# Finer pieces in an instruction planner, first scores in two PSUM banks behind products of ones, and embeddings taken first

## Chip, cores and metric

The kernel runs on one core of a Trainium2 chip. The metric is the device time of one execution in microseconds (us), the median of three runs; less is better. TensorE (PE in the profile) multiplies matrices, VectorE (DVE) and ScalarE (ACT) work on vectors, GpSimd (POOL) and SyncE (SP) mostly start transfers.

## What is computed

Three stages on 4608 tokens of 512 numbers. The first is attention between `x` (8 batches, 8 heads, 512 positions, 64 numbers) and a small `state` (32 positions), read in both directions. The second is a feed-forward layer with a squared ReLU. The third sends each token to one of 8 experts and scales the result by a softmax weight.

```python
scores = scale * np.matmul(x, state.transpose(0, 1, 3, 2))
a = softmax(scores);  xread = np.matmul(a, state)
scores2 = scale * np.matmul(state, x.transpose(0, 1, 3, 2))
a2 = softmax(scores2);  sread = np.matmul(a2, x)
tok = concatenate([xread, sread])            # 8 x (512 + 32) tokens of 512
h = relu(tok @ w_in);  y = (h * h) @ w_out   # 512 -> 2048 -> 512
logits = norm(y) @ norm(expert_emb).T / tau
e = argmax(logits);  gate = softmax(logits)[e]
out = gate * (relu(y @ w1[e]) @ w2[e])       # 512 -> 1024 -> 512
```

`w_in` and `w_out` arrive as 64-bit floats and are turned into 32-bit ones in the kernel.

## The kernel before, in words

Every product that decides the routing has to be more exact than one 16-bit product, so most operands are split into a high and a low 16-bit half and multiplied as high-high, high-low, low-high.

**Decoding.** `w_in` and `w_out` come in 16 blocks (`block`, eight of each). A block is 1 MB of 64-bit numbers. `to_f32` decodes it with one instruction of 1024 elements on ACT (L882) and three on DVE (L885, L887, L894); `wi_scale` squares a `w_in` block on ACT (L911), sums the squares with four products with a matrix of ones (`oneb`, L919) and takes a power-of-two scale from the sum (L925, L932). Two blocks give one quarter of `w_in`.

**Attention of batch 0** (`first_attention`, `first_scores`, `first_scale`). It starts before any weight is there. `first_scores` multiplies two halves of `x` with the state, both into one PSUM tile `S` (L597, eight 32-bit products for a half, each issued as two passes with a weight load each). `weigher` makes the softmax: row maxima (L519), subtraction (L521), exponential on ACT (L528), sum (L530), three small steps, multiplication (L536), a cast on ACT (L540), the low half (L542), and a transposing DMA (L549). `state_side` does the other direction (L750 and on).

**Hidden layer.** For batch b, `first_state_w` or `state_w` multiplies the state with a quarter of `w_in` (L649, L686) and splits the result into `sw` (L659 on ACT, L316 on DVE). `up1` multiplies `sw` with the transposed softmax (L1349 to L1351, twelve products of 256 columns for a hidden unit, in a ring of two PSUM tiles `u`); `hidden` reads `u` on ACT (L1302), squares it and splits it. `down1` multiplies the hidden values with `w_out`: for the first two token groups in 32 bits (L1412, 16 products for each of 4 tiles, so 64; it can begin before the halves of `w_out` exist), later in 16-bit halves (L1433 to L1435). It has a ring of two PSUM tiles `d`: the first two tiles must be read by `route_tile` (L1173, then L321 and L316) before the third begins.

**Order.** Nothing is scheduled by a compiler. Each piece of work is a Python generator that yields requests such as `"pe", 1.2` (engine, duration), events, or slots. `Plan.run` keeps a clock for each engine, takes again and again the request that can start first (ties go to the lower priority number), and lets that generator write its instructions. Each engine then executes its list strictly in order. After a request a generator's own time is the end plus `LAT`:

```python
dep = r[2] if len(r) > 2 else th[2]
key = (max(dep, self.free[r[0]]), th[1])
th[2] = start + dur + self.LAT
```

So the size of a request sets how finely two products' lists can be mixed: `down1` asks for four 32-bit products (which the planner counts as 16; the trace shows two passes for each), or for twelve 16-bit ones, in one request.

**Embeddings.** `embeddings` normalises the expert embeddings: 22 small DVE instructions (L1138 to L1159), one of them behind four small products (L1146). It starts after `wo scale`, that is after all 16 blocks are decoded. Its two inputs are loaded by `prepare` on SP's queue.

## Time and profile before

| | |
|---|---|
| median of 3 runs | 1090.7 us (1090.12 to 1091.49) |
| the profiled execution, its own time | 1089.88 us |
| its span, first to last instruction | 1088.1 us |
| PE busy | 1039.9 us (96%) |
| DVE busy | 684.6 us (63%) |
| ACT busy | 588.2 us (54%) |

The profile gives for each engine what it executed and when. A row of the timeline has the start, the duration, the engine, the line, what is written from what, and in brackets how long the engine was idle before and what ended that. [...]

### The profile page before, as it was taken

The numbers are of one execution on the slowest core, as the hardware profiler recorded it, in microseconds if no ns is written. First come the engines' busy times: TensorE is split into PE (matmuls) and PEld (weight loads), VectorE is DVE, ScalarE is ACT, GpSimd is POOL, SyncE is SP. The second block draws the span as 40 slices with busy tenths as digits, with TensorE's granted clock in tenths as the row PEclk, the third lists the DMA queues.
The fourth block names the chain that finished last, engine by engine and source line by source line (L and its number), as shares of the span: only waits on it lengthen the run. The fifth ranks groups of instructions, "written<-read, shape, count | busy, mean of one in ns | idle before, by whom it ended". The sixth has DMA issues, their size and how long they took to land. (4 is left out here: it accounts for less than half of the span.)

```text
span 1088.1 us, 26339 instructions
## 1 busy us (share of the span) xinstructions
PE 1039.9 (96%) x10657; PEld 672.2 (62%) x10657; DVE 684.6 (63%) x1787; ACT 588.2 (54%) x976; POOL 124.3 (11%) x149
## 2 busy tenths in 40 slices
PE   4679999999999999999999999999999999999997
PEld 3345446565656566565555666677677777767774
DVE  5788798868878778887797784466322323222222
ACT  4778779787887988887787984211110101111110
POOL 0000000200101001002002020312122121212111
PEclk8799999999999999999999999999999999999999
DMA  6873144874875565887559587753898777694691
GB/s 216 288 248 110 60 97 146 233 209 133 242 226 150 153 181 173 233 210 217 166 162 262 194 262 246 218 138 80 277 285 166 195 226 219 169 292 141 182 311 69
DMA packets 161311, 211.74 MB, mean 195 GB/s; under 512 B 112225, under 2 KB 114529, under 8 KB 155938
## 3 DMA queue, kind: packets, MB, share of 16 engines
q1 hardware_dynamic: 152866, 182.94, 58.2%
q0 software_dynamic: 8320, 27.08, 8.2%
q8 instruction: 85, 1.39, 0.5%
q14 instruction: 40, 0.33, 0.1%
HBM read 257.92 MB, written 51.68 MB: 285 GB/s over the span
## 5 line engine op out<-in xcount | busy, mean ns | idle before, releaser
L1699 ACT ACTIVATE r<-u 128x512 f32<-128x512 f32 x70 | 41.8, 597 | 319.5 <-PE u L1745 288.7
L1433 PE MATMUL d<-wo_t,g 128*128 128x512 f16 x480 | 182.1, 379 | 1.0 <-DVE g L1319 1.0
L1435 PE MATMUL d<-wo_t,g 128*128 128x512 f16 x480 | 182.1, 379 | 0.2
L1434 PE MATMUL d<-wo_t,g 128*128 128x512 f16 x480 | 182.1, 379 | 0.0
L1349 PE MATMUL u<-aT,sw 128*128 128x256 f16 x512 | 141.3, 276 | 9.7 <-ACT r L1302 7.6
L1351 PE MATMUL u<-aT,sw 128*128 128x256 f16 x512 | 141.0, 275 | 0.2 <-DVE sw L316 0.2
L1350 PE MATMUL u<-aT,sw 128*128 128x256 f16 x512 | 141.0, 275 | 0.0
L1702 DVE CAST hh<-r 128x512 f16<-128x512 f32 x70 | 29.9, 428 | 127.8 <-ACT r L1699 126.3
L1302 ACT ACTIVATE r<-u,cg 128x512 f32<-128x512 f32 x120 | 81.5, 680 | 47.9 <-PE u L1351 27.2
L1713 DVE TENSOR_SCALAR o<-d,rec,wo_t 128x512 f32<-128x512 f32 x35 | 28.3, 810 | 111.0 <-PE d L1768 108.5
L1275 POOL DMA_INDIRECT rec_d<-rec,pi x34 | 38.5, 1132 | 519.9 <-DVE is L301 140.8
L1768 PEld LDWEIGHTS <-hh 128*128 128x128 f16 (+1 forms) x688 | 54.7, 103 | 57.6 <-issue 1.3
L1321 DVE TENSOR_TENSOR g<-r,g 128x512 f16<-128x512 f32 x120 | 82.2, 688 | 7.5 <-ACT r L1316 5.9
L1435 PEld LDWEIGHTS <-g 128*128 128x128 f16 x480 | 46.9, 98 | 57.7 <-DVE g L1321 1.2
L1743 PE MATMUL u<-xes,stage 128*128 128x128 f16 x448 | 75.9, 219 | 0.0
L1745 PE MATMUL u<-xes,stage 128*128 128x128 f16 x448 | 75.9, 219 | 0.0
L1744 PE MATMUL u<-xes,stage 128*128 128x128 f16 x448 | 75.9, 219 | 0.0
L1433 PEld LDWEIGHTS <-g 128*128 128x128 f16 x480 | 47.2, 98 | 46.3 <-DVE g L1319 1.9
L1316 ACT ACTIVATE r<-r 128x512 f32<-128x512 f32 x120 | 74.5, 626 | 1.4
L1434 PEld LDWEIGHTS <-g 128*128 128x128 f16 x480 | 46.9, 98 | 44.2
L1743 PE MATMUL u<-xes,xx 128*128 128x128 f16 x416 | 70.5, 220 | 0.0
L1744 PE MATMUL u<-xes,xx 128*128 128x128 f16 x416 | 70.4, 219 | 0.0
(338 smaller groups left out, 2637.7 us busy)
## 6 DMA issues: line engine op xcount, KB each, us to landing
w_d<-he SPq DMA_DIRECT2D x128, 256.0 KB
g<-w_d SPq DMA_DIRECT2D x16, 2048.0 KB
wo_t<-w_d SPq DMA_DIRECT2D x16, 2048.0 KB
stage<-w_d SPq DMA_DIRECT2D x14, 2048.0 KB
he<-w_d SPq DMA_DIRECT2D x14, 2048.0 KB
xx<-w_d SPq DMA_DIRECT2D x13, 2048.0 KB
sw<-w_d SPq DMA_DIRECT2D x13, 2048.0 KB
stage<-in_w_dram SPq DMA_DIRECT2D x20, 1024.0 KB
```

The costliest lines, as they stand in the source:

```text
L1302: nc.scalar.activation(out=r, in_=ps, func=AF.Relu, scale=cg[:, g:g + 1] if u >= F32U else cgq[:, c:c + 1])
L1316: nc.scalar.activation(out=r, in_=r, func=AF.Square)
L1321: V.tensor_tensor(out=gl, in0=r, in1=gh, op=ALU.subtract)
L1349: mm(o, lhsT=hl[:, i, 0, fs], rhs=aT[:, i, :], start=i == 0, stop=False)
L1350: mm(o, lhsT=hl[:, i, 0, fs], rhs=aT[:, 2 + i, :], start=False, stop=False)
L1351: mm(o, lhsT=hl[:, i, 1, fs], rhs=aT[:, i, :], start=False, stop=i == 1)
L1433: mm(ps, lhsT=g_h[:, f, ts], rhs=w[:, 0, :], start=f == 0, stop=False)
L1434: mm(ps, lhsT=g_h[:, f, ts], rhs=w[:, 1, :], start=False, stop=False)
L1435: mm(ps, lhsT=g_l[:, f, ts], rhs=w[:, 0, :], start=False, stop=f == KF - 1)
L1743: mm(p[:, j, xs], lhsT=w[:, 0, k, fs], rhs=xe[:, k, xs], start=k == 0, stop=False)
L1744: mm(p[:, j, xs], lhsT=w[:, 0, k, fs], rhs=xe[:, 4 + k, xs], start=False, stop=False)
L1745: mm(p[:, j, xs], lhsT=w[:, 1, k, fs], rhs=xe[:, k, xs], start=False, stop=k == 3)
```

## The change

It does these things, all of them before or around the first 130 us of the program, and by the planner everywhere:

- `Plan`: a request of a generator for the same engine as its last one is no longer delayed by `LAT`; the DMA queue is taken to begin at 1.2.
- `down1` asks for its products in pieces: a quarter of what it asked for at a time, in both forms.
- `first_attention` issues five products of a 128x128 matrix of ones with 512 columns of ones before it waits for the state, and four more before the scores (`warm`), into one of the `d` tiles, which it releases again.
- `first_scores` puts the two halves into two tiles of the `u` ring instead of the one tile `S`; `weigher` takes the tile and a function that releases it.
- `embeddings` is started at the program's begin, loads its inputs on ACT's queue ahead of everything else there, and asks for its DVE work in six pieces.
- The priority of `first_scale` goes from 0.95 to 1.2.

```diff
--- before.py
+++ after.py
@@ -115,12 +115,12 @@
 
     def __init__(self):
         self.free = dict.fromkeys(("pe", "act", "dve", "pool", "sp"), 0.0)
-        self.dma_free = 0.0
+        self.dma_free = 1.2
         self.threads = []
         self.cur = None
 
     def add(self, gen, prio):
-        th = [gen, prio, self.cur[2] if self.cur else 0.0, None]
+        th = [gen, prio, self.cur[2] if self.cur else 0.0, None, None]
         self.threads.append(th)
         was, self.cur = self.cur, th
         self._advance(th)
@@ -141,10 +141,13 @@
 
     def _advance(self, th):
         was, self.cur = self.cur, th
+        at = th[2]
         try:
             th[3] = next(th[0])
         except StopIteration:
             self.threads.remove(th)
+        if th[2] != at:
+            th[4] = None
         self.cur = was
 
     def run(self):
@@ -163,7 +166,7 @@
                         self._advance(th)
                         break
                 else:
-                    dep = r[2] if len(r) > 2 else th[2]
+                    dep = r[2] if len(r) > 2 else th[2] - (self.LAT if r[0] == th[4] else 0)
                     if r[0] == "pe" and 1.3 <= th[1] < 5:
                         dep += self.MARGIN
                     key = (max(dep, self.free[r[0]]), th[1])
@@ -174,7 +177,7 @@
                 (start, _), th, dep = best
                 eng, dur = th[3][0], th[3][1]
                 self.free[eng] = start + dur
-                th[2] = start + dur + self.LAT
+                th[2], th[4] = start + dur + self.LAT, eng
                 self._advance(th)
 
 
@@ -502,13 +505,12 @@
                 ss_ = slice(sb * 128, sb * 128 + 128)
                 for n, (a, w) in enumerate(pairs):
                     mm(o, lhsT=w[:, c, ss_], rhs=a[:, c, :], start=n == 0, stop=n == 2)
-        w = weigher(b, Sp, xh, xl, scl, 0, 32)
-        yield from w
-
-    def weigher(b, Sp, xh, xl, scl, m0, m1):
+        S4 = Sp.rearrange("p a (h n) -> p (a h) n", n=NS)
+        yield from weigher(b, S4, xh, xl, scl, 0, 32, s_slots.release)
+
+    def weigher(b, S4, xh, xl, scl, m0, m1, read):
 
         ms, n = slice(m0, m1), NS * (m1 - m0)
-        S4 = Sp.rearrange("p a (h n) -> p (a h) n", n=NS)[:, ms]
         mx = small.tile([128, 32], F32, name="mx")[:, ms]
         e1 = xh.rearrange("p c s -> p (c s)").bitcast(F32).rearrange("p (m n) -> p m n", n=NS)
         a16 = xl.rearrange("p c s -> p (c s)").rearrange("p (t c m n) -> p t m c n", t=2, c=4, n=NS)
@@ -519,11 +521,7 @@
         V.tensor_reduce(out=mx, in_=S4, axis=X, op=ALU.max)
         yield dve(n)
         V.tensor_tensor(out=e1, in0=S4, in1=mx.unsqueeze(2).to_broadcast([128, m1 - m0, NS]), op=ALU.subtract)
-        ev("S read", b, m1).set()
-        if m1 == 32:
-            if m0:
-                yield ev("S read", b, m0)
-            s_slots.release()
+        read()
         yield act(n)
         nc.scalar.activation(out=e1, in_=e1, func=AF.Exp, scale=scl)
         yield dve(n)
@@ -559,6 +557,16 @@
 
     def first_attention():
 
+        yield d_slots
+        idle, k_d = ps_d.tile([128, 512], F32, name="d"), d_slots.last()
+
+        def warm(n):
+            yield "pe", 0.25 * n
+            for _ in range(n):
+                mm(idle.rearrange("p (a n) -> p a n", a=4), lhsT=oneb, rhs=oneb.unsqueeze(1).to_broadcast([128, 4, 128]),
+                   start=True, stop=True)
+
+        yield from warm(5)
         yield ev("st", 0)
         stt = st_t.pop(0)
         yield xhl_slots
@@ -571,11 +579,13 @@
         yield "pe", 0.2
         mm(p[:, 2:3], lhsT=one32, rhs=ss[:, 2:3], start=True, stop=True)
         mm(p[:, 256:512], lhsT=oneb, rhs=xl.bitcast(BF16)[:, :, :64], start=True, stop=True)
-        yield s_slots
-        Sp = ps_s.tile([128, 4, 256], F32, name="S")
+        at = plan.now()
+        yield from warm(4)
+        d_slots.release(k_d)
+        plan.cur[2] = at
         for t in range(2):
-            plan.add(first_scores(t, Sp, xh, xl, stt), 0.4 + 0.1 * t)
-        plan.add(first_scale(ss, stt), 0.95)
+            plan.add(first_scores(t, xh, xl, stt), 0.4 + 0.1 * t)
+        plan.add(first_scale(ss, stt), 1.2)
         v = small.tile([128, 2], F32, name="sv")[:, 0:1]
         yield tiny(4)
         V.tensor_scalar(out=v, in0=p[:, 2:3], scalar1=FLOOR, scalar2=None, op0=ALU.max)
@@ -588,16 +598,22 @@
         plan.add(first_state_w(stf), 0.6)
         plan.add(group_bound(0, p), 0.7)
 
-    def first_scores(t, Sp, xh, xl, stt):
+    def first_scores(t, xh, xl, stt):
         yield ev("first x", t)
         xf = xf_t[0, 0]
-        yield "pe", 2.0
-        for sb in (2 * t, 2 * t + 1):
+        at = plan.now()
+        yield u_slots
+        plan.cur[2] = max(at, plan.now())
+        Sp, k_h = ps_u.tile([128, 512], F32, name="u").rearrange("p (a n) -> p a n", a=2), u_slots.last()
+        yield "pe", 1.9
+        for a in range(2):
+            sb = 2 * t + a
             for c in range(4):
-                mm(Sp[:, sb, c * 64:c * 64 + 64], lhsT=xf[:, c, sb * 128:sb * 128 + 128], rhs=stt[:, c, :],
+                mm(Sp[:, a, c * 64:c * 64 + 64], lhsT=xf[:, c, sb * 128:sb * 128 + 128], rhs=stt[:, c, :],
                    start=True, stop=True)
         ev("scored", t).set()
-        yield from weigher(0, Sp, xh, xl, eighth, 16 * t, 16 * t + 16)
+        S4 = Sp.rearrange("p a (h n) -> p (a h) n", n=NS)
+        yield from weigher(0, S4, xh, xl, eighth, 16 * t, 16 * t + 16, lambda: u_slots.release(k_h))
 
     def first_scale(ss, stt):
 
@@ -1132,10 +1148,13 @@
         ev("experts").set()
 
     def embeddings():
-        yield ev("wo scale")
-        yield ev("prepared")
-        yield "dve", 3.0
+        yield "act", 1.0
+        nc.scalar.dma_start(emf, embT)
+        nc.scalar.dma_start(tsb, tau.to_broadcast([128, 1]))
+        plan.cur[2] += 2.5
+        yield tiny(1)
         V.reciprocal(out=itau, in_=tsb)
+        yield tiny(2)
         V.tensor_scalar(out=itau, in0=itau, scalar1=float(2.0 ** -14), scalar2=None, op0=ALU.mult)
         e2 = small.tile([128, 4, NE], F32, name="emq", bufs=1)
         V.tensor_tensor(out=e2, in0=emf, in1=emf, op=ALU.mult)
@@ -1144,12 +1163,16 @@
         yield "pe", 0.4
         for k in range(4):
             mm(p[:, 0:NE], lhsT=one32, rhs=e2[:, k, :], start=k == 0, stop=k == 3)
-        yield tiny(20)
+        yield tiny(1)
         v = small.tile([128, NE], F32, name="env", bufs=1)
         V.tensor_scalar(out=v, in0=p[:, 0:NE], scalar1=FLOOR, scalar2=None, op0=ALU.max)
         t_slots.release()
         y = small.tile([128, NE], F32, name="eny", bufs=1)
+        yield tiny(5)
+        yield tiny(6)
         rsqrt(y, v, NE)
+        yield tiny(4)
+        yield tiny(4)
         V.tensor_tensor(out=y, in0=y, in1=v, op=ALU.mult)
         V.tensor_scalar(out=y, in0=y, scalar1=1e-6, scalar2=None, op0=ALU.add)
         V.reciprocal(out=y, in_=y)
@@ -1406,9 +1429,9 @@
             for q in range(NB):
                 yield ev("f32", q)
                 yield ev("g", u, q)
-                yield pe(16, 512)
                 for i in range(2):
                     for f in range(2):
+                        yield pe(4, 512)
                         mm(pair[i][0], lhsT=g32[:, i, 2 * q + f, 128 * u:128 * u + 128], rhs=wo32[q][:, f, :],
                            start=q + f == 0, stop=q == NB - 1 and f == 1)
                 ev("down32", u, q).set()
@@ -1427,8 +1450,8 @@
                     if u == F32U:
                         for a in (2 * q, 2 * q + 1):
                             yield ev("wo", a)
-                    yield pe(12, 512)
                     for f in range(4 * q, 4 * q + 4):
+                        yield pe(3, 512)
                         w = wo[f // 2][:, :, f % 2, :]
                         mm(ps, lhsT=g_h[:, f, ts], rhs=w[:, 0, :], start=f == 0, stop=False)
                         mm(ps, lhsT=g_h[:, f, ts], rhs=w[:, 1, :], start=False, stop=False)
@@ -1820,9 +1843,8 @@
         yield from load(cs, cst, 1 << 17)
         yield from load(cs16, cst16, 1 << 16)
         yield from load(rid, rowid, 1 << 15)
-        yield from load(tsb, tau.to_broadcast([128, 1]), 512)
-        t = yield from load(emf, embT, 1 << 14)
-        yield "pool", 1.0, t
+        t = plan.now()
+        yield "pool", 1.0, t + 2.0
         dz = mg.tile([128, REC], F32, name="rec0", bufs=1)
         nc.gpsimd.memset(dz, 0.0)
         nc.gpsimd.tensor_copy(dz[:, 513:514].bitcast(I32), rid[:, NT:NT + 1])
@@ -1831,6 +1853,7 @@
 
     def start():
         plan.add(first_attention(), PRIO_A0)
+        plan.add(embeddings(), 0.9)
         yield from load_st(0)
         yield from load_x(0, 0)
         yield from block(0)
@@ -1839,7 +1862,6 @@
             plan.add(attention(b), 1.15 if b == 1 else PRIO_A1)
         plan.add(loader(), 1)
         plan.add(prepare(), 1)
-        plan.add(embeddings(), 3)
         plan.add(up1(), 5)
         plan.add(down1(), 5)
         plan.add(moe2(0, NMAIN), 5)
```

The rows below are the instruction lists of an engine as the built programs have them (runs of equal rows merged; line numbers of the program in question, those of the changed one are higher by 3 to 23; a line of dots stands for rows left out that repeat).

TensorE at the program's begin: the sums of the state's squares (t), the scores, and the other direction's scores. Before:

```order
L572 MATMUL t<-ss,one_95 128x1
L573 LDWEIGHTS oneb
L573 MATMUL t<-xx,oneb 128x256
L597 MATMUL S<-stt,xx 128x64 x16
L750 MATMUL t<-xx,stt 64x512 x4
```

Changed:

```order
L566 LDWEIGHTS oneb
L566 MATMUL d<-oneb 128x512
...
L580 MATMUL t<-ss,one_95 128x1
L581 LDWEIGHTS oneb
L581 MATMUL t<-xx,oneb 128x256
...
L612 MATMUL u<-stt,xx 128x64 x16
L1165 MATMUL t<-emq,one_95 128x8 x4
L766 MATMUL t<-xx,stt 64x512 x2
L635 MATMUL t<-ss,one_95 128x2
```

Five products of ones stand ahead of all, four between the sums and the scores; the embeddings' products follow the scores, and half of the other direction's scores is put off.

TensorE after the first 48 products of the hidden layer, around the sums of squares of the second pair of `w_in` blocks (u from pjk) and the first products of `down1` (d from wo_t, g). Before:

```order
L1351 MATMUL u<-aT,sw 128x256
L919 LDWEIGHTS oneb
...
L619 MATMUL t<-ss,one_95 128x2
...
L919 MATMUL u<-pjk,oneb 128x256
L649 MATMUL S<-wi,sthl 32x256 x16
L1412 MATMUL d<-wo_t,g 128x512 x4
L1349 LDWEIGHTS sw
```

Changed:

```order
L1374 MATMUL u<-aT,sw 128x256
L1435 MATMUL d<-wo_t,g 128x512
L935 LDWEIGHTS oneb
...
L935 MATMUL u<-pjk,oneb 128x256
L1435 MATMUL d<-wo_t,g 128x512
L665 MATMUL S<-wi,sthl 32x256 x16
L1435 MATMUL d<-wo_t,g 128x512
L935 LDWEIGHTS oneb
...
L935 MATMUL u<-pjk,oneb 128x256
L1435 MATMUL d<-wo_t,g 128x512 x5
```

The first 32-bit products of `down1` now stand one by one between the sums of squares and the state products instead of behind them in groups of four. Further on, 24 of the 64 (16 before) stand ahead of the sums for batch 1 (L467 before, L470 in the changed program).

TensorE at the end of the first two tiles of `down1` and the begin of the third. Before, the last group of the first 32 products is followed by batch 1's state scores, twelve hidden products and the embeddings' products:

```order
L1412 MATMUL d<-wo_t,g 128x512 x4
L750 LDWEIGHTS sthl
L750 MATMUL t<-xx,sthl 64x512
...
L1349 LDWEIGHTS sw
L1349 MATMUL u<-aT,sw 128x256
...
L1146 MATMUL t<-emq,one_95 128x8 x4
L1412 MATMUL d<-wo_t,g 128x512 x8
```

Changed (the first L1435 row ends with the 29th product, the second with the 32nd; the last begins the third tile):

```order
L1435 MATMUL d<-wo_t,g 128x512 x5
L1047 MATMUL t<-fv,one_95 128x1
L766 LDWEIGHTS sthl
L766 MATMUL t<-xx,sthl 64x512
...
L1435 MATMUL d<-wo_t,g 128x512 x3
L766 LDWEIGHTS sthl
L766 MATMUL t<-xx,sthl 64x512
...
L1435 MATMUL d<-wo_t,g 128x512 x3
```

Six state-score products now stand among the last products of the first two tiles, and between the 32nd product and the third tile only six others are left.

## Rows read from the trace of the kernel before

**Rows 1.** page: engines' busy time, and granted clock in 40 slices

```profile
PE 1039.9 (96%) x10657; PEld 672.2 (62%) x10657; DVE 684.6 (63%) x1787; ACT 588.2 (54%) x976; POOL 124.3 (11%) x149
...
PEclk8799999999999999999999999999999999999999
```

**Rows 2.** busy time by stretch; columns in the first line

```profile
core 0: us, PE busy (x) PEld busy (x) DVE busy (x) ACT busy (x) POOL busy (x), PEclk, DMA share, GB/s
0.00:28.00 28.00, 12.79 (x51) 9.25 (x51) 16.19 (x36) 12.75 (x17) 1.23 (x10) 0.83 0.66 213
28.00:48.00 20.00, 11.37 (x92) 7.28 (x90) 15.54 (x29) 16.10 (x23) 0.18 (x1) 0.76 1.02 377
...
64.00:84.00 20.00, 13.18 (x129) 7.68 (x128) 17.13 (x32) 16.93 (x28) 0.00 (x0) 0.90 0.85 253
84.00:115.00 31.00, 30.70 (x204) 17.75 (x202) 24.24 (x60) 25.10 (x38) 0.00 (x0) 0.95 0.38 140
...
121.00:700.00 579.00, 570.68 (x4869) 341.77 (x4868) 464.89 (x1272) 456.20 (x772) 48.13 (x62) 1.00 0.66 190
```

**Rows 3.** waits of PE by line: us in total, times, longest

```profile
PE u L919 <- ACT pjk L911: 16.6, 5, 5.5
PE u L1349 <- ACT r L1302: 7.6, 11, 1.8
PE t L467 <- ACT xx L461: 4.9, 1, 4.9
```

**Rows 4.** timeline, first 13 us: start us, us, engine, line

```profile
0.76 1.28 ACT L568 ACT_TABLE_LOAD   x1 [0.76 <-PEq L1883]
0.77 0.41 SPq L338 DMA_DIRECT2D stt<-in_stT_dram  x1
...
1.04 0.20 POOL L353 MEMSET oneb<- 128x128 bf16 x1
...
2.93 0.42 ACT L568 ACTIVATE xx<-stt 128x256 bf16<-128x256 f32 x1 [0.89 <-DMA stt<-in_stT_dram]
...
4.00 0.37 PE L573 MATMUL t<-xx,oneb 128*128 128x256 bf16 x1
...
5.54 7.06 PE L597 MATMUL S<-stt,xx 128*128 128x64 f32 x32 [1.17 <-DMA xx<-in_xT_dram]
...
12.64 0.69 DVE L519 TENSOR_REDUCE mx<-S 128x16 f32<-128x512 f32 x1 [5.84 <-PE S L597]
```

**Rows 5.** source lines L597 and L1412, weight loads: ns least/median/most

```profile
L597 PEld LDWEIGHTS S<-stt,xx x32: 285/334/334, 5.5 to 12.1; 128*128 128x128 f32 x32
...
L1412 PEld LDWEIGHTS d<-wo_t,g x128: 186/190/338, 50.2 to 151.7; 128*128 128x128 f32 x128
```

**Rows 6.** timeline of DVE: embeddings, first and last of 18

```profile
118.97 0.15 DVE L1149 TENSOR_SCALAR env<-t 128x8 f32<-128x8 f32 x1
...
122.67 0.19 DVE L1159 TENSOR_TENSOR en_l<-emq,en_h 128x32 f16<-128x32 f32 x1
```

**Rows 7.** timeline of PE, 43 to 59 us

```profile
43.89 0.60 PE L919 MATMUL u<-pjk,oneb 128*128 128x256 bf16 x4 [3.26 <-ACT pjk L911]
...
50.23 4.95 PE L1412 MATMUL d<-wo_t,g 128*128 128x512 f32 x8
...
55.67 3.60 PE L1412 MATMUL d<-wo_t,g 128*128 128x512 f32 x8
```

**Rows 8.** timeline of PE, 80 to 84 us

```profile
80.20 0.59 PE L467 MATMUL t<-ss,one 128*128 128x3 f32 x2 [4.90 <-ACT xx L461]
```

**Rows 9.** timeline of DVE: the last block's last decoding step

```profile
101.20 1.22 DVE L894 SCALAR_TENSOR_TENSOR wo_t<-stage 128x1024 int32<-128x1024 int32 x1
```

**Rows 10.** timeline of PE, 108 to 126 us

```profile
108.30 3.60 PE L1412 MATMUL d<-wo_t,g 128*128 128x512 f32 x8
111.82 0.84 PE L750 MATMUL t<-xx,sthl 128*64 128x512 f16 x6
...
116.66 8.83 PE L1412 MATMUL d<-wo_t,g 128*128 128x512 f32 x16 [1.79 <-DVE rec L316]
```

## The prediction

> **What bounds the kernel now.** I read the page first, then busy time by stretch, then the waits, then the timelines. The page shows PE busy for 1039.9 us of 1088.1 [rows 1]: 48.2 us of idle time are all that a better order can win, apart from stretches at the lower clock. The stretches say where that time lies [rows 2]: 28 − 12.8 = 15.2 us before 28 us, 8.6 from 28 to 48, 6.8 from 64 to 84. From 84 to 115 only 0.3 us is left and from 121 to 700, 579.0 − 570.7 = 8.3 us. So PE is full from 84 us on, and there a microsecond of PE time saved is one off the end, unless something else holds PE up.
>
> What PE waits for is mostly the decoding chain [rows 3]: 16.6 us in five waits of L919 for the square of a `w_in` block, 4.9 us once at L467. DVE, which does three of the four decoding steps, is busy for 17.1 of 20 us in the stretch 64 to 84 [rows 2]. So ahead of 84 us decoding sets the pace. The waits of the hidden products for `u` are 7.6 us in eleven [rows 3].
>
> At the beginning the scores of batch 0 take PE from 5.54 to 12.60, 0.22 us for each of 32 passes, and DVE, idle for 5.84 us, reads only when all are done [rows 4]. The clock is the lower one there: the weight loads of this line last 334 ns, those of L1412, with the same 128x128 of 32 bits, 190 at the median and 338 at most [rows 5].
>
> **The beginning.** `oneb` is set at 1.24 us [rows 4]. [...] `x` is there at 5.54 [rows 4], so 0.6 us is lost if the clock stays low. If it is at its higher level by then, the loads go from 334 to 190 ns [rows 5], the pace of 0.22 us to about 0.11, and the 16 passes of the first half end at 6.1 + 16 × 0.11 = 7.9. Since the first half has its own bank, DVE starts then: 12.64 − 7.9 = 4.7 us earlier. At the lower clock it starts at 6.1 + 3.5 = 9.6, 3.0 earlier, by the bank alone.
>
> The embeddings take this back. Their 18 DVE steps span 122.86 − 118.97 = 3.9 us [rows 6], three more stand ahead of them, and all now precede the first decoding step. If they lie wholly on DVE's path, 4.7 − 3.9 leaves 0.8; if DVE would have stood idle, all 4.7 is kept; if the chain of small steps delays more than itself, decoding is 1 us later. I take 0.5 earlier: decoding follows these steps on the same queue. The place they leave, 119 to 123 us, lies beside PE's run from 116.66 to 125.49 [rows 10] and costs or wins nothing there. The two loads moved to ACT's queue cost two issues (0.41 us on SP): the table load begins at 1.58 instead of 0.76 and ends at 2.86, just ahead of the state's landing at 2.93 [rows 4]. That is hidden with 0.07 us to spare; if not, it is 0.4 at most. SP loses two issues behind the first block, where nothing waits for them.
>
> **The finer pieces.** Two passes, one product, take 3.60 / 4 = 0.90 us [rows 7]. Three now stand around the sums of squares from 40 to 48, where PE waits 3.26 us at once [rows 7]: 2.7 us. Eight more (24 instead of 16) stand ahead of L467, which waits for 4.90 us [rows 8]: 7.2 us, of which the stretch's 6.8 can be filled. So up to 9.5 us of work moves into idle time; the lower bound is nothing, if each piece itself waits for its hidden unit and holds up L919 behind it.
>
> Decoding caps this. The last step ends at 101.20 + 1.22 = 102.4 [rows 9], 101.9 with the 0.5 from above. The four products that need this block follow, 3.60 us [rows 7], and six state scores stand among them, 0.84 [rows 10]: the 32nd product ends at 106.3 at the earliest; before, it ends at 111.82 [rows 10], 5.5 us later. The offer of 9.5 exceeds that, so I take the cap; even half the offer, with the front's 0.5, comes to 5.3.
>
> **The third tile.** It starts 116.66 − 111.82 = 4.84 us after the 32nd product, since both tiles of the ring must be read first; that chain is unchanged. Before, PE filled all but 1.79 us of it [rows 10]; now only six state scores (0.84) remain, so about 4 us idle. It starts at 106.3 + 4.84 = 111.2 instead of 116.66: 5.5 us earlier, and 0.84 us of state scores that came later is already done. Hence **−6.3 us**.
>
> What I cost at nothing: the lower clock behind this idle time (8.83 us for 16 passes at 116.66, against 2 × 3.60 [rows 7, 10], so 1.6 us that the kernel has already; a longer gap may cost as much again, or nothing); the low stretch at 50.23 (4.95 us against 3.60 [rows 7]), which pieces in the gap may spare, since the cap hides it; and the changed order from 121 us on, bounded by −8.3 (all idle time there) and, nothing in the rows excluding a loss, +8.
>
> **Sum.** 1089.88, the profiled execution's own time, − 6.3 = 1083.6. The median lies 0.8 above that execution: **1084.4 us**.
>
> **A rule on the clock.** The passes of L597 are 7 us of nearly unbroken work, and their loads stay at 334 ns [rows 4, 5]; so not every work raises the clock, and ones of 512 columns are another load than 64. [...]
>
> **Rivals.**
> - *The clock is not up in time.* The first half comes at 9.6, decoding ends 1.7 later, and so does everything up to the third tile: 1086.1. For it: L597's loads [rows 5]. [...] Chance 0.11.
> - *Weight loads keep their length at either clock*, so the scores gain only the bank: also 1086.1. L1412's loads of 190 and 338 ns speak against it [rows 5]. Chance 0.02. [...]
> - *The gaps only move.* PE works strictly in order: a piece that waits for its hidden unit holds up the sum of squares behind it, and with it the scale, the halves and the next quarter. Then at most about 2 us is won: 1088.7. For it: the 16.6 us of waits belong to ACT and DVE, which are given no less work [rows 3]. Against: the 32 products end 9.4 us after the last decoding step today, so PE, not decoding, is late there [rows 9, 10]. Chance 0.16.
> - *Later waits go too.* With every piece a quarter as long, the planner could fill most of the 8.3 us from 121 to 700 [rows 2]: about 7 less, 1077.4. Chance 0.10.
> - *Slower: the ring of `u`.* With the finer pieces the order gathers hidden products into longer runs (24 and 18 in a row, where 6 and 12 alternated with other products). `u` has two tiles, and a run that is faster than ACT reads waits at each further tile: 7.6 / 11 = 0.69 us each [rows 3]. Nine such waits eat the 6.3 us; two for each of eight batches are 16 × 0.69 = 11.0, so 1084.4 + 11.0 = 1095.4. Against: from 121 to 700 PE idles for 8.3 us in 579 with such runs already among the others [rows 2]. Chance 0.11.
>
> **Chances.** The forecast, 1080 to 1088.4, has 0.50. A measurement of this kernel tells about 0.2% (2.2 us) from no change. Faster by more than that, below 1088.5: the forecast 0.50, the two rivals at 1086.1 0.13, the later waits 0.10 and 0.05 of the gaps' 0.16, together 0.78. Within 0.2%: the other 0.11 of the gaps. Slower: 0.11. **Range** 1076 to 1090.5: the low end holds the later waits and most of the unknown 4.2 us by which decoding could come earlier still; the high end holds the gaps that only move, with nothing won at all. Left out are the slower case and the far ends, some 0.16.
>
> **What would show each step.** The first L519 starts near 7.9 us if the clock is up, near 9.6 if not, and L597's line has loads of 190 or 334 ns. All embedding steps on DVE end before 22 us. PE's idle time falls from 8.6 to about 6 between 28 and 48 and from 6.8 to 1 or less between 64 and 84; the last L894 step ends near 102; the 32nd product ends near 106, the third tile starts near 111 after some 4 us of idle time. The total of waits for `r` stays near 7.6 us; at 14 or more the ring decides. The forecast is wrong if the last decoding step comes more than 2 us from 102, if L919 waits behind pieces of `down1`, or if PE's idle time beyond 121 us differs from 8.3 by more than 3.

## The result and the profile after

The changed kernel takes 1106.4 us (median of four runs, 1105.39 to 1110.16), the kernel before 1091.0 (1090.12 to 1091.49) beside it: a ratio of 1.0148, 95% interval 1.0124 to 1.0173. It is slower by 15.4 us where 6.3 less was forecast. The profiled execution is one of 1105.39 us.

The page after, in the lines of [rows 1] (the first row counts the span's busy time of each engine; PEclk is the granted clock of each slice, in tenths of the full one):

```profile
PE 1046.8 (95%) x10666; PEld 672.7 (61%) x10666; DVE 689.3 (62%) x1779; ACT 603.3 (55%) x984; POOL 124.3 (11%) x149
...
PEclk6798899999999999999999999999999999999999
```

PE is idle for 1103.5 − 1046.8 = 56.7 us (48.2 before) and busy for 6.9 us more; the nine products of ones are 2.31 + 1.81 = 4.1 of these. So both parts grew: 8.5 us of idle time, and slower or added products. Where, the stretches tell (columns as in [rows 2]):

```profile
28.00:48.00 20.00, 14.39 (x92) 8.14 (x91) 18.20 (x25) 17.11 (x23) 0.18 (x1) 0.67 0.72 256
...
64.00:84.00 20.00, 19.46 (x163) 11.93 (x162) 18.34 (x29) 19.07 (x30) 0.00 (x0) 1.00 0.82 258
84.00:115.00 31.00, 22.47 (x151) 11.13 (x149) 26.67 (x65) 25.77 (x41) 0.00 (x0) 0.89 0.43 159
...
121.00:700.00 579.00, 565.26 (x4813) 338.27 (x4812) 453.04 (x1205) 467.07 (x777) 47.68 (x62) 0.99 0.66 185
```

Up to 84 us the forecast came true: idle time fell from 8.6 to 5.6 us between 28 and 48 and from 6.8 to 0.5 between 64 and 84. Then the 31 us that were full before [rows 2] have 8.5 us of idle time, and the stretch to 700 us has 13.7 instead of 8.3.

A better measure than busy time is the **lead**: add up PE's products, each with the median distance to the next one of its kind in the kernel before, and ask when the other kernel has done as much (worked out from all PE rows of the two traces; minus is ahead of the kernel before, us).

| at (us of the kernel before) | 90 | 100 | 110 | 120 | 160 | 220 | 700 | 1000 |
|---|---|---|---|---|---|---|---|---|
| changed kernel | −11.2 | −9.3 | −4.5 | +0.4 | −2.0 | +6.8 | +10.6 | +15.8 |

At 90 us PE was 11.2 us ahead; the forecast offered 9.5 and let 5.5 of them reach the 32nd product. Thirty microseconds later all of it was gone, and another 15 were lost behind that. The waits of PE by line name the places (us in total, times, longest; L935 was L919, L1372 was L1349, L1435 was L1412, L1219 was L1196; `rec` and `f` are steps of the reading of a `d` tile, `xr` is such a reading transposed by DMA for the routing products):

```profile
PE u L935 <- ACT pjk L927: 15.3, 5, 9.9
PE t L1219 <- DMA xr<-rec: 8.3, 7, 1.9
PE d L1435 <- DVE rec L319: 5.8, 1, 5.8
PE u L1768 <- issue: 4.4, 1, 4.4
PE u L1372 <- ACT sw L675: 3.8, 2, 2.7
PE d L1456 <- DVE rec L319: 3.3, 1, 3.3
PE d L1456 <- DVE f L1200: 2.8, 1, 2.8
...
PE u L1372 <- ACT r L1325: 0.8, 2, 0.5
```

The waits for `r`, which my slower rival counted on, fell from 7.6 [rows 3] to 0.8 us. Waits for the `d` ring, one of 1.79 us before [rows 10], are now three of 5.8, 3.3 and 2.8.

PE where the lead was lost (timeline; rows left out are alike):

```profile
93.72 0.39 PE L1372 MATMUL u<-aT,sw 128*128 128x256 f16 x1 [2.69 <-ACT sw L675]
...
95.06 0.39 PE L1374 MATMUL u<-aT,sw 128*128 128x256 f16 x1 [0.73 <-DVE sw L319]
...
102.35 4.46 PE L1435 MATMUL d<-wo_t,g 128*128 128x512 f32 x10
...
108.02 2.84 PE L1435 MATMUL d<-wo_t,g 128*128 128x512 f32 x6
110.79 0.84 PE L766 MATMUL t<-xx,sthl 128*64 128x512 f16 x6
117.44 2.08 PE L1435 MATMUL d<-wo_t,g 128*128 128x512 f32 x2 [5.81 <-DVE rec L319]
```

PE waits 2.69 and 0.73 us for the last quarter's `sw`, runs its hidden products for `u` behind that (0.42 us each up to 97.8, at a granted clock of 0.50, and 0.27 later, at 1.00; the lower clock here and below means the first of the two), works with no gap over 0.15 us from 95.06 to 110.86, and waits 5.81 us for the third tile. The list has no other product ahead of either wait; f4_held below, which keeps 24 hidden products back for the second, fills that one.

### The profile page after: what moved, and what is told of

Same layout as the page of the kernel before. It is cut to its first block, busy times and chain, and to the rows that moved or that the text cites. A ratio compares the mean times of both kernels' runs of the same rounds, so it can differ in the third digit from the quotient of the medians.

```text
span 1103.5 us, 26325 instructions
## 1 busy us (share of the span) xinstructions
PE 1046.8 (95%) x10666; PEld 672.7 (61%) x10666; DVE 689.3 (62%) x1779; ACT 603.3 (55%) x984; POOL 124.3 (11%) x149
## 5 line engine op out<-in xcount | busy, mean ns | idle before, releaser
L1372 PE MATMUL u<-aT,sw 128*128 128x256 f16 x512 | 141.8, 277 | 4.6 <-ACT sw L675 3.8
L1768 PE MATMUL u<-xes,stage 128*128 128x128 f16 x448 | 76.0, 219 | 0.0
L1768 PE MATMUL u<-xes,xx 128*128 128x128 f16 x416 | 70.3, 219 | 0.0
```

The costliest lines, as they stand in the source:

```text
L1372: mm(o, lhsT=hl[:, i, 0, fs], rhs=aT[:, i, :], start=i == 0, stop=False)
L1768: mm(p[:, j, xs], lhsT=w[:, 1, k, fs], rhs=xe[:, k, xs], start=False, stop=k == 3)
```

## The experiments

What was in question: do the finer pieces, the `LAT` rule or the beginning lose the time; is it the lower clock; or does any order that the planner makes anew lose, whatever the edit? All ratios are to the kernel before on the same chip, whose own median differed from chip to chip, from 1090.4 to 1103.6 us.

**The parts, each planned anew.** `e1_coarse` is the changed kernel with the old sizes of requests, `e2_nolat` is it without the `LAT` rule, `e3_pieces` and `e4_lat` are the kernel before with only the pieces or only the rule, `e5_front` is the beginning alone.

From the changed kernel, e1_coarse (in `down1`; e5_front has this edit and the next):

```diff
+                yield pe(16, 512)
                 for i in range(2):
                     for f in range(2):
-                        yield pe(4, 512)
...
+                    yield pe(12, 512)
                     for f in range(4 * q, 4 * q + 4):
-                        yield pe(3, 512)
```

From the changed kernel, e2_nolat (in `Plan.run`; e4_lat has its reverse, with the lines on `th[4]` of the change, from the kernel before):

```diff
-                    dep = r[2] if len(r) > 2 else th[2] - (self.LAT if r[0] == th[4] else 0)
+                    dep = r[2] if len(r) > 2 else th[2]
```

e3_pieces is the reverse of the first of these diffs, in the kernel before.

> The changed kernel with the products of down1 asked for in the old sizes (four 32-bit or twelve 16-bit products in one request); all else as changed. Theory A (the finer pieces spend PE's stock of ready products before 90 us, so that PE stands idle at the last quarter of w_in, at the third tile and at 165 us): the loss goes, 1087 to 1092 us, and PE idles for under 2 us between 84 and 115. Theory B (the planner's rule on LAT does it): no change, 1103 to 1109. Theory C (the embeddings and the new beginning do it): no change, 1103 to 1109.

> The changed kernel without the planner's rule that a generator's next request for the same engine isn't delayed by LAT; all else as changed. Theory A (finer pieces): no change within 3 us, 1103 to 1109. Theory B (that rule): back at 1087 to 1092. Theory C (the beginning): 1103 to 1109.

> The kernel before with the finer pieces of down1 alone. Theory A: slower by most of the loss, 1098 to 1108, with PE idle for 4 us or more between 84 and 121. Theory B and theory C: 1086 to 1092. The step of the prediction that the pieces fill gaps: 1084 to 1087.

> The kernel before with the planner's rule on LAT alone. Theory A and theory C: 1088 to 1093. Theory B: 1098 to 1108.

> The new beginning alone (ones, two banks, embeddings first, the moved loads): the changed kernel with down1's old sizes and without the planner's rule on LAT. Theory D (each of the two planner changes costs by itself, the beginning wins a little: the pairs run so far differ by 0.2 to 0.35% with and without it): 2 to 5 us faster than the kernel before. Theory C (the beginning is part of the loss): 3 us or more slower. The prediction's step of 0.5 us, fully covered by decoding: within 1 us.

| kernel | ratio | 95% interval |
|---|---|---|
| e1_coarse (rule + beginning) | 1.0367 | 1.0337 to 1.0397 |
| e2_nolat (pieces + beginning) | 1.0113 | 1.0086 to 1.0139 |
| e3_pieces | 1.0135 | 1.0106 to 1.0163 |
| e4_lat | 1.0402 | 1.0372 to 1.0431 |
| e5_front | 1.0052 | 1.0035 to 1.0068 |

Every part alone loses, and they don't add up: the rule costs 4.0% alone and nothing that stands out beside the pieces (1.0148 with both and the beginning, 1.0113 without the rule; the changed kernel itself came to 1.0100 on another chip, below). The waits of PE with the rule alone:

```profile
PE u L1352 <- DMA aT<-xx: 12.5, 4, 6.3
PE t L1199 <- DMA xr<-rec: 10.3, 3, 5.6
PE u L1746 <- DMA xx<-w_d: 8.8, 1, 8.8
PE S L689 <- DVE sw L319: 8.2, 4, 4.4
PE d L1415 <- DVE rec L319: 6.6, 1, 6.6
```

`aT`, `xx` and `sw` for the state products are not among the changed kernel's waits, `xr` and `rec` are, at other sizes. Which wait costs most differs from loser to loser, but one place recurs: PE waits 4.5 to 10.0 us for a block of the expert stage's weights (`xx<-w_d`, as in the third line) in six of the nine new orders measured here (e1_coarse, e2_nolat, e3_pieces, e4_lat, e7_p16, f4_held), and not in the changed kernel, e5_front or the control.

**The two forms of piece, and a control.** `e6_p32` and `e7_p16` change one of the two requests in the kernel before; `e8_control` is the kernel before.

In e6_p32:

```diff
-                yield pe(16, 512)
                 for i in range(2):
                     for f in range(2):
+                        yield pe(4, 512)
```

In e7_p16:

```diff
-                    yield pe(12, 512)
                     for f in range(4 * q, 4 * q + 4):
+                        yield pe(3, 512)
```

> The kernel before with only the 32-bit products of down1 asked for one by one; the 16-bit ones in twelves as before. Theory A1 (the 32-bit pieces spend PE's stock before the last quarter of w_in is decoded): most of the loss of the finer pieces, 8 to 15 us slower than the kernel before, PE idle for 6 us or more from 84 to 121. Theory A2 (the 16-bit pieces, later, do it): within 3 us of the kernel before.

> The kernel before with only the 16-bit products of down1 asked for in threes; the 32-bit ones in fours as before. Theory A1: within 3 us of the kernel before. Theory A2: 8 to 15 us slower, with PE idle for 12 us or more beyond 160 us where the kernel before idles for some 6 up to 700.

> The kernel before, unchanged, for its trace on the same chip as the others. All theories: no difference from itself (within 0.3%). If a chip with slower loads makes PE wait for weights of the expert stage near 730 us here too, those waits aren't the change's.

Measured: 1.0265 (1.0244 to 1.0286), 1.0215 (1.0194 to 1.0236) and 1.0002 (0.9985 to 1.0018). Either form alone loses more than both together (1.0135, on another chip). Busy time by stretch, of the control, of e6_p32 and of e7_p16 in that order (PE first):

```profile
0.00:84.00 84.00, 54.80 (x354) 32.89 (x355) 64.29 (x122) 58.57 (x84) 3.22 (x17) 0.79 0.72 243
84.00:121.00 37.00, 35.02 (x212) 19.61 (x211) 28.57 (x77) 30.66 (x48) 0.00 (x0) 0.96 0.35 125
121.00:700.00 579.00, 567.69 (x4853) 340.43 (x4852) 462.53 (x1260) 454.97 (x772) 45.19 (x62) 1.00 0.64 189
```

```profile
0.00:84.00 84.00, 59.98 (x400) 36.19 (x401) 64.16 (x120) 60.01 (x89) 4.38 (x17) 0.84 0.71 243
84.00:121.00 37.00, 26.43 (x225) 13.31 (x222) 33.56 (x68) 29.00 (x42) 0.00 (x0) 0.90 0.32 118
121.00:700.00 579.00, 555.66 (x4622) 327.27 (x4623) 440.20 (x1197) 451.23 (x765) 41.54 (x55) 0.98 0.62 173
```

```profile
84.00:121.00 37.00, 35.05 (x211) 19.51 (x210) 28.56 (x77) 30.95 (x48) 0.00 (x0) 0.97 0.35 122
121.00:700.00 579.00, 558.18 (x4786) 334.71 (x4785) 454.04 (x1207) 454.11 (x767) 40.57 (x57) 0.99 0.62 183
```

The 32-bit pieces are what fills PE ahead of 84 us (+5.2) and empties it from 84 to 121 (−8.6): more is lost than was moved. The 16-bit ones leave the first 121 us alone and lose 9.5 us up to 700. The forecast had given them no loss.

**The same work with the order held.** Here the new instructions are written inside requests that exist already, so that the planner's clocks, and with them the order of all else, stay those of the kernel before. In the traces of f0_banks, f1_begin, f2_clock and f3_both the order on PE, ACT, DVE and POOL is row by row that of the kernel before, but for the added ones. `f0_banks` is the two halves in two tiles of the `u` ring alone, `f1_begin` that and the nine ones, `f2_clock` the kernel before with ones in two known gaps, `f3_both` the last two together. `f4_held` is another thing: the changed kernel, planned anew, with two hidden units kept back to fill the third tile's wait.

f0_banks has `first_scores` and `weigher` of the change, with the request left at 2.0. f1_begin adds five products ahead of the sums of the state's squares, and four, written alike, ahead of the first half:

```diff
         yield "pe", 0.2
+        for _ in range(5):
+            mm(p.rearrange("p (a n) -> p a n", a=4), lhsT=oneb, rhs=oneb.unsqueeze(1).to_broadcast([128, 4, 128]),
+                   start=True, stop=True)
         mm(p[:, 2:3], lhsT=one32, rhs=ss[:, 2:3], start=True, stop=True)
```

f2_clock has the same ahead of L467 (and seven ahead of L1146):

```diff
         yield "pe", 0.2
+        for _ in range(18 if b == 1 else 0):
+            mm(p.rearrange("p (a n) -> p a n", a=4), lhsT=oneb, rhs=oneb.unsqueeze(1).to_broadcast([128, 4, 128]),
+               start=True, stop=True)
         mm(p[:, 0:3], lhsT=one32, rhs=ss, start=True, stop=True)
```

f4_held, in `up1` of the changed kernel:

```diff
+            if (u, c) in ((1, 6), (1, 7)):
+                yield ev("down32", 0, NB - 1)
             at = plan.now()
             yield u_slots
```

> The kernel before with the score halves in two banks alone, no ones, order unchanged. By the prediction's step for the lower clock DVE begins at 9.0 to 9.6 us and the weight loads of the scores stay at 334 ns; 1 to 3 us of lead on the kernel before up to the third tile.

> The kernel before with the ones (five and four products, not told to the planner) and the score halves in two banks, the embeddings where they were: the order of all other instructions on all engines is that of the kernel before. Theory D (the work of the new beginning is good, the new order that the planner makes of it loses): DVE begins near 8.5 instead of 12.6 us, PE stays ahead through the third tile, 2.5 to 4 us faster than the kernel before. Theory F (whatever comes early meets the third tile's wait and is lost there): within 1 us.

> The kernel before with products of ones in two of PE's idle gaps, 18 ahead of the sums for batch 1 (near 75 us) and 7 ahead of the embeddings' products (near 114 us), not told to the planner, the order of all else unchanged. If the lower clock behind these gaps costs what the rows suggest (4.33 us against 2.6 for 24 hidden products, 8.83 against 7.2 for 16 passes): 2 to 3 us faster. If PE then only waits longer at the next step: within 1 us. If the ones hold up what stands behind them: 1 to 3 us slower.

> Both of the two former edits. If they add up: 4.5 to 7 us faster than the kernel before. If the earlier beginning already fills the gaps so that the ones stand in the way: no better than the beginning alone.

> The changed kernel, where the last two hidden units of the first two groups (24 products) are held back until the 32nd product of down1 has been issued, so that PE has them for the wait before the third tile; the planner makes a new order of the rest. Theory A (the pieces use up PE's stock and leave that wait uncovered): PE idles for 3.5 us or less before the third tile, where the changed kernel idles for 5.8, and the run takes 3 to 8 us less than the changed kernel, a ratio of 1.007 to 1.012 to the kernel before. Theory G (each new order of the plan costs one to four per cent, wherever its waits fall): no such gain, 1.015 or more.

| kernel | ratio | 95% interval | lead at 100, 260, 1000 us |
|---|---|---|---|
| f0_banks | 0.9985 | 0.9968 to 1.0002 | |
| f1_begin | 1.0001 | 0.9987 to 1.0016 | −3.6, −2.6, −1.0 |
| f2_clock | 1.0000 | 0.9986 to 1.0015 | |
| f3_both | 0.9969 | 0.9954 to 0.9984 | −6.1, −5.7, −4.6 |
| f4_held | 1.0297 | 1.0270 to 1.0324 | |

The first L518 or L521 of DVE, which reads the first half of the scores, in the changed kernel, in f1_begin and in f0_banks:

```profile
8.60 0.69 DVE L521 TENSOR_REDUCE mx<-u 128x16 f32<-128x512 f32 x1 [1.37 <-PE u L612]
```

```profile
7.68 0.69 DVE L518 TENSOR_REDUCE mx<-u 128x16 f32<-128x512 f32 x1 [1.00 <-PE u L603]
```

```profile
8.89 0.69 DVE L518 TENSOR_REDUCE mx<-u 128x16 f32<-128x512 f32 x1 [2.11 <-PE u L595]
```

It started at 12.64 [rows 4]. The bank alone brings 3.75 us, the ones 1.2 more in this execution; in two others with the same nine ones the first half came at 10.00 (g2_emb) and 10.55 (g1_after), later than with the bank alone. In f1_begin the third tile starts at 113.02 instead of 116.66 [rows 10], so 3.6 us reach that point; but by 1000 us 2.6 of them are gone, and the median doesn't move. One execution tells such a lead only to a few microseconds: in two executions of f3_both the third tile starts at 110.58 and (h1_f3) at 114.31. Only with ones in the later gaps as well do the medians fall, by some three microseconds: f3_both is the one of these kernels that is faster. Of f4_held the third tile's wait is gone, as meant, and other waits are there (waits of PE):

```profile
PE t L1219 <- DMA xr<-rec: 15.7, 8, 6.5
PE u L1768 <- DMA xx<-w_d: 10.0, 1, 10.0
```

**The changed kernel again, and the rest with the order held.** `g1_after` is the changed kernel, `g2_emb` f1_begin with the embeddings ahead of decoding, `g3_hoist` f3_both with six products of `down1` written into the gaps at 36 to 44 us; `h1_f3` and `h2_g3` repeat f3_both and g3_hoist on one chip.

g2_emb has the loads on ACT's queue at the begin, the four small products behind the scores, and the DVE work (`emb_c`) in `to_f32`, ahead of the first decoding step on DVE:

```diff
             yield dve2(1024) + (at,)
+            if "p" in early:
+                emb_c()
             V.tensor_scalar(out=lo, in0=lo, scalar1=29, scalar2=None, op0=ALU.logical_shift_right)
```

g3_hoist has one product in `first_scale`, and five in `wi_scale`, and leaves them out in `down1`:

```diff
         yield pe(4, BW)
+        if q in (2, 3):
+            hoist(4 if q == 2 else 1)
         for k in range(4):
             mm(p[:, 0:BW], lhsT=oneb, rhs=sq[:, k, :], start=k == 0, stop=k == 3)
```

> The changed kernel, unchanged, on the chip of the other three: does its loss repeat place by place? If the 4.4 us near 975 us, for which the profile names no releaser, belongs to the change, it is there again at the same products; if it is chance, it is elsewhere or gone. PE idle for 5 to 7 us before the third tile and for 3 us or more near 165 and near 208 us in either case; 1.012 to 1.018 of the kernel before.

> The kernel f1 (ones and two banks, order else unchanged) with the embeddings put ahead of all decoding and their loads on ACT's queue, not told to the planner: all other instructions keep their order. The prediction's step (3.9 us of DVE lie on its path and take the gain of the beginning back but for 0.5): the last decoding step near 102 us, 2.5 to 4 us later than in f1, and 1 to 4 us slower than f1. If DVE would have stood idle: as f1 within 1 us.

> The kernel f3 (ones, two banks, ones in two gaps) with six of the 32-bit products of down1 moved forward, four ahead of the sums of squares of the second pair of blocks, one ahead of L619 and one ahead of the next sums, not told to the planner: all other instructions keep their order, and nothing else is asked for in finer pieces. If a piece in an idle gap is worth its time (the prediction's step of 0.90 us each): 3 to 5 us faster than f3, about 0.993 of the kernel before. If decoding sets the pace there and the gap only moves (to the sums for batch 1): as f3 within 1 us, with 3 us or more of added idle time between 62 and 80 us. If the pieces hold up the sums of squares: slower than f3 by 1 us or more.

> The kernel f3 again (ones, two banks, ones in two gaps; order else unchanged), beside the next one on one chip: 0.995 to 0.998 of the kernel before if its first result (0.9969) holds.

> The kernel g3 again (f3 with six products of down1 moved into idle gaps), beside f3 on one chip. If a piece in an idle gap is worth its time: 3 us or more faster than f3. If decoding sets the pace and the gap only moves: within 2 us of f3.

| kernel | ratio | 95% interval |
|---|---|---|
| g1_after | 1.0100 | 1.0080 to 1.0120 |
| g2_emb | 1.0031 | 1.0015 to 1.0047 |
| g3_hoist | 0.9942 | 0.9921 to 0.9962 |
| h1_f3 | 0.9978 | 0.9963 to 0.9994 |
| h2_g3 | 0.9974 | 0.9958 to 0.9989 |

The waits of g1_after are the same ones: for `rec` 5.7 and 3.4, for `f` 2.8, and 4.4 at L1768. So the places belong to the order, not to one execution. Its size is 1.0 to 1.5% by chip.

The last decoding step of the last block (DVE, L906 there, L901 in f1_begin) starts at 103.86 in g2_emb and at 97.56 in f1_begin, 6.30 earlier. Of that, 10.00 − 7.68 = 2.3 are the scores (the first 16 passes took 1.90 us in f1_begin, all 32 took 7.06 in that execution of g2_emb), and 4.0 the embeddings. f0_banks, on the chip of g2_emb, has this step at 98.08 and the first half at 8.89: by the same count the embeddings cost 4.7.

g3_hoist and f3_both side by side, busy time by stretch, h1_f3 first, h2_g3 second:

```profile
28.00:48.00 20.00, 12.34 (x90) 7.88 (x90) 15.45 (x28) 17.69 (x25) 1.49 (x6) 0.67 0.92 346
48.00:64.00 16.00, 14.90 (x70) 7.68 (x55) 13.90 (x24) 11.84 (x19) 0.98 (x2) 0.94 0.47 147
64.00:84.00 20.00, 17.28 (x154) 10.10 (x152) 18.31 (x33) 16.11 (x25) 0.00 (x0) 0.91 0.73 239
```

```profile
28.00:48.00 20.00, 15.19 (x102) 8.65 (x100) 15.74 (x30) 17.60 (x25) 2.47 (x7) 0.90 0.82 309
48.00:64.00 16.00, 13.68 (x54) 7.42 (x55) 13.85 (x20) 11.84 (x18) 0.00 (x0) 0.79 0.56 169
64.00:84.00 20.00, 16.77 (x154) 10.07 (x153) 18.10 (x34) 15.58 (x26) 0.00 (x0) 0.91 0.74 254
```

The moved products fill 2.9 us from 28 to 48; 1.2 of it is missing from 48 to 64 and 0.5 from 64 to 84. The first execution of f3_both has more in these stretches than h1_f3:

```profile
28.00:48.00 20.00, 13.31 (x91) 7.81 (x91) 15.51 (x28) 17.73 (x25) 2.66 (x7) 0.69 0.79 298
48.00:64.00 16.00, 15.71 (x66) 8.66 (x65) 14.08 (x21) 11.84 (x19) 0.00 (x0) 0.96 0.59 173
```

Against it the pieces fill 1.9 us, and 2.0 are missing directly behind. The two medians are 1087.66 and 1087.19 us. With all other order held, six earlier pieces are worth about 0.5 us, which these runs can't tell from nothing. The 0.9942 of g3_hoist on another chip did not come again: its repetition h2_g3 gave 0.9974.

**Taken together.** Ten measurements are of nine kernels planned anew, the changed one twice: every one is slower, by 0.5 to 4.0%. The six kernels with the order held lie between −0.6 and +0.3%. That is not yet proof that the new order as such is to blame in each: for the beginning, g2_emb loses 0.31% with the order held and e5_front 0.52% planned anew, and their intervals overlap. Of the pieces only six were tried with the order held, and of the rule none.

## Why the prediction was wrong

**Right.** The first half's scores came at 8.60 (7.9 forecast); the embeddings cost decoding 4.0 to 4.7 us where the order is held (3.9 forecast), so that the last decoding step ends at 101.34 + 1.23 = 102.57 (near 102), no gain; all embedding work on DVE ends at 22.4. The idle time of 28 to 84 us went as forecast. Of the 0.7 us by which the first half missed, 0.5 is `x`: taken to be there at 5.54 as before, it let the scores begin at 6.59 and not at 6.1. With the embeddings loaded first, the scores begin behind a wait for `x` at 6.59, 6.87 (g1_after) and 6.32 (g2_emb); in the kernel before and f0_banks they begin at 5.54 and 5.21. Of the terms of the 7.9, no run shows the 6.1 us at which the nine ones were to end, nor the pace of 0.11 us: both were estimates of mine. In the changed kernel the five ones end at 1.30 + 2.31 = 3.61, the four at 4.19 + 1.81 = 6.00, and the 16 passes of the first half take 1.97 us, 0.12 each. Both cases of the first half, near 7.9 and near 9.6, are seen, within 1.0 us: the same products ended it at 8.60 in one execution and, in g1_after, at 10.55 (timeline of DVE):

```profile
10.55 0.69 DVE L521 TENSOR_REDUCE mx<-u 128x16 f32<-128x512 f32 x1 [3.30 <-PE u L612]
```

The loads in front of it last 333 ns at the median, against 192 in the first execution. What decides between the two isn't shown.

**First failed step: what follows the last decoding step.** The prediction let "the four products that need this block follow, 3.60 us, and six state scores stand among them, 0.84", and had the 32nd product end at 106.3. It ended at 108.02 + 2.84 = 110.86, 0.96 ahead of the kernel before. The decoding time was right; but I took PE to be through with all else by then. The cap of 106.3 was worked out from the last block of `w_out` alone. PE was 11 us ahead at 90 and so came early to work that wasn't ready: the last quarter's `sw`. That hangs on the last block of `w_in`, whose last decoding step is no earlier than it was (timeline of DVE, before and after):

```profile
87.81 1.22 DVE L894 SCALAR_TENSOR_TENSOR wo_t<-stage 128x1024 int32<-128x1024 int32 x1
87.91 1.23 DVE L910 SCALAR_TENSOR_TENSOR wo_t<-stage 128x1024 int32<-128x1024 int32 x1
```

It ends at 89.14 (89.03 before), and its square, sums and scale are still to come before `sw`. Products of `down1` that stood here before are among those moved to the earlier gaps. So from 95.06 a backlog of 15.8 us stood ahead of the 32nd product, not 4.4. This is the rival "the gaps only move" as a mechanism, with decoding as the end of the chain, and f3_both and g3_hoist, with their repetitions, show it on a smaller scale with nothing else changed.

**Second: the third tile.** "That chain is unchanged", at 4.84 us; it took 117.44 − 110.86 = 6.58. The reading of the tile is queued on ACT behind the scaling of a `w_in` half, itself behind another wait (timeline of ACT):

```profile
111.27 0.60 ACT L707 ACTIVATE sw<-S 128x512 f16<-128x512 f32 x1 [1.95 <-DVE sw L319]
111.76 1.14 ACT L970 ACTIVATE wi<-wi,swi 128x1024 f16<-128x1024 f32 x1
112.80 0.68 ACT L1196 ACTIVATE rec<-d,ends 128x512 bf16<-128x512 f32 x1
```

The reading starts 1.9 us after the 32nd product's end. In the kernel before it started ahead of that end (111.82), with the first of the two tiles (timeline of ACT):

```profile
111.27 0.68 ACT L1173 ACTIVATE rec<-d,ends 128x512 bf16<-128x512 f32 x1
```

I had counted what PE lost from this place, the hidden products, and not what stands ahead on ACT. The third tile came at 117.44, not at 111.2, and 0.8 later than before.

**Third: the order from 121 us on, costed at nothing**, with −8.3 and +8 as bounds. It lost about 15 us by the lead (from +0.4 to +15.8), nearly twice the upper one. The prediction's own sign of failure, idle time beyond 121 us off by more than 3, is there: 13.7 against 8.3. Two waits for the `d` ring are part of it, 3.34 and 2.81 us at 169 and 212 us, each followed by products at the lower clock. Behind the first a product takes 0.63 us at a granted clock of 0.50, and 0.38 from 173.04 on, at 1.00; behind the second it takes 0.38 at first and 0.63 from 215.82 to 217.1. The first (timeline of PE):

```profile
169.41 0.42 PE L1456 MATMUL d<-wo_t,g 128*128 128x512 f16 x1 [3.34 <-DVE rec L319]
169.63 0.63 PE L1457 MATMUL d<-wo_t,g 128*128 128x512 f16 x1
...
173.04 0.38 PE L1456 MATMUL d<-wo_t,g 128*128 128x512 f16 x1
```

The waits for `xr`, 8.3 us in seven, and the one of 4.42 at L1768 are further parts. The experiments say that this term could not have been zero with a small range: each of nine new orders lost, and the losses behind 121 us were of up to 12 us in one stretch (567.69 − 555.66 in e6_p32). Nor does the premise hold that behind 84 us "a microsecond of PE time saved is one off the end": of the 3.6 us that f1_begin brings to the third tile, 1.0 is left at 1000 us.

**The slower rival** had the right sign and the wrong place. It put the loss on the `u` ring; it is the `d` ring, the reading queues of ACT and DVE, and transfers. Its chance of 0.11 was too small for an edit that reorders the whole program.

**Open.** Why the planner's new orders lose at these places is argued, not shown: I take its clocks for ACT and DVE to differ from the chip's, and the order of before to fit the chip by more than the planner knows. The `LAT` rule has no version with the order held, and a third `d` tile was not tried. Where f1_begin's lead goes between 200 and 1000 us is not known. g2_emb and f1_begin are compared across two chips. The last decoding step starts at 95.12 in one execution of f3_both and at 98.84 in the other, so the 4.0 and 4.7 us of the embeddings are rough.

The best version is f3_both: 0.9969 and, repeated, 0.9978. Of the change it keeps the two banks and the ones; pieces, rule and embeddings it leaves out, and ones in two gaps are added.

## What to carry to other kernels

An edit of a scheduler's rules or sizes is a new schedule of the whole program, and its cost is not that of the places where the rows look better. Test such an edit first with the order held, by writing the new instructions inside old requests; if that brings nothing (here 0.5 us for six of the pieces), the gain that the planner promises isn't there. Before filling a gap with later work, ask what that work was covering: here the wait that it left open came at 111.6 us and lasted 5.81, and the first six passes behind it took 5.00 us, at a granted clock of 0.50 up to 121.5.

## What the hardware showed that was not expected

- Nine products of ones don't settle how long the passes of the scores take. In the changed kernel's first execution the first half took 1.97 us and the second 3.31 (PE, timeline). In f1_begin and f3_both, with as many ones, a half took 1.90 to 2.00 us; in g1_after and g2_emb the 32 passes took 7.06 together, as in f0_banks, which has no ones:

```profile
6.59 1.97 PE L612 MATMUL u<-stt,xx 128*128 128x64 f32 x16 [0.59 <-DMA xx<-in_xT_dram]
8.76 3.31 PE L612 MATMUL u<-stt,xx 128*128 128x64 f32 x16 [0.19 <-DMA xx<-in_xT_dram]
```

  Loads of 192 ns at the median in that execution stand against 333 in g1_after, the same program. For g1_after the granted clock from 6 to 14 us is given as 1.00, beside these loads: here I go by the durations, not by that column.
- Behind ones in a gap the products were quick in some executions and slow in others, and quick without ones too. The third tile's 16 passes took 8.83 us [rows 10] in the kernel before and 7.13 in f3_both, with seven ones ahead of them. But they took 7.13 as well in f0_banks and in f1_begin, with no ones in this gap and the same wait of 1.79 (timeline of PE):

```profile
113.02 7.13 PE L1419 MATMUL d<-wo_t,g 128*128 128x512 f32 x16 [1.79 <-DVE rec L316]
```

  So no gain of these seven is shown. Behind the wait of L467, 14 hidden products took 0.42 us in the kernel before (at a granted clock of 0.50) and 22 in f1_begin, without ones there; with ones it was none in f3_both and 13 in g3_hoist.
- PE stood still for 4.4 us in front of one product with no releaser in the profile, in both executions of this program, on two chips; f4_held and e1_coarse have such a stop too, of 4.9 and 4.2, among the same products. In the changed kernel's first execution the granted clock was 1.00 ahead of it (970 to 974.4 us) and 0.50 behind it (979.1 to 981.7), and the next products took 0.24 us instead of 0.19. From 974 to 980 us the instruction queue moved one packet; that this is the cause isn't shown.

```profile
979.07 0.21 PE L1768 MATMUL u<-xes,g 128*128 128x64 f16 x1 [4.42 <-issue]
```
